# The last inverse stage of a long convolution with 64 output columns per weight: high and low constants side by side, low halves added in memory by accumulating GpSimd transfers

## The chip, the cores and the metric

The kernel runs on one core of a Trainium2 chip. The metric is the device time of one execution in microseconds (us), shown as the median of three runs. A profile is one more execution with the hardware profiler on. TensorE is PE in the rows (PEld is its weight load), VectorE is DVE, ScalarE is ACT, GpSimd is POOL, and SyncE, which only issues transfers here, is SP.

## What is computed

Four layers act on x (2048 rows, 576 columns), each with a residual and a row normalization ahead of it. Layers one and three are a Fourier mix; layers two and four multiply by the output of a branch that depends on the inputs k, v and the filters alone, so that it is computed once.

```
x = x + real(DFT_seq(DFT_hidden(layernorm(x))))       # dense DFT matrices
x = x + layernorm(x) * y                              # y: the branch
x = x + real(DFT_seq(DFT_hidden(layernorm(x))))
x = x + layernorm(x) * y

kv = conv4(k, shift_k) * v
y  = irfft(rfft(kv, 4096) * rfft(ssm_k, 4096))[:2048] + kv * ssm_D
```

## The kernel before

**Numbers.** All matrix products run on values rounded to a shorter mantissa (type fp32r). To keep the precision each operand is split into a high and a low part, and a product takes three matmuls: high by high, high by low, low by high. `split` (lines 97 to 99) makes the two parts: ACT copies the rounded high part, DVE subtracts.

**The main work.** `layer` (line 300) multiplies by the sequence DFT in 128 steps of 14 matmuls of 512 columns, with constants that are loaded and split as it goes (`load_c`, line 213; a ring of three buffers). Behind each block of 512 outputs come eight pieces of `hidden` (line 276), each 27 matmuls of 288 columns. The second Fourier layer is done by `strassen` and is not touched.

**The branch.** `branch` (line 349) is a generator. It is advanced between the parts of the first Fourier layer, by estimated costs (`work`, `total`, `spent`, lines 769 to 798): a row of the last stage counts `I2_COST` = 2.0 us. It has three stages. The first transforms (`f1_products`) and writes to memory (`t_d`). The middle takes 64 groups: `mid_half` transforms again, `mid_kernel` and `mid_signal` form the complex product in the columns of two tiles (`kk` and, before, a scratch tile `p2`), `mid_inverse` transforms back, evicts into a buffer of the ring `vo` and stores to `v_d`. The last stage, `i2_products` (line 551), makes 32 row tiles, 16 for each half of the 576 columns. One such **row** reads a tile of 128 partitions by 2 by 288 from `v_d`, splits it (`split_feed`, line 586), multiplies it with the constants `i2c` of this row, evicts 128 by 288 with one activation into a buffer of `vo` (three buffers, also used by the middle stage) and stores it to `yb_d` from the ACT queue.

**Where the rows stand.** The list `feeds` (lines 562 to 569) sets the order: 32 groups of the first half, groups of the second half with the first ten rows put between them (two groups to a row, from group 37 on), and then the last 22 rows without a group between them. The first stretch is called the mixed stretch below, the second the late stretch. After the last group `fc` and `land`, the rings of constants and of loaded tiles, go from two buffers to four (lines 634 to 643).

**What orders the engines.** The program is written as one list and a scheduler puts each engine's instructions into a fixed order; within an engine they run in that order. The function `act` (line 509) ties every ScalarE operation of the branch behind the previous one. Waits on buffers are semaphores. The constants of a row are loaded by `load_fr` (line 170) from GpSimd's queue, because that transfer also rounds. PSUM for the branch and for `hidden` are three banks in rotation (`bank`, line 83).

**Who reads the result.** `gated` (line 656) loads `yb_d[j]` from SP's queue for the second layer, and again for the fourth.

Of the kernel before, what the change touches and what calls it, by code (L numbers as in the profile page):

```python
# [10 lines left out]
F32 = mybir.dt.float32  # L11
# [4 lines left out]
P = 128  # L16
HP = P // 2
S = 2048
# [47 lines left out]
def fnet_h3_kernel(ctx: ExitStack, tc: tile.TileContext, x, c_mat, w_re, w_im, k_pad, v, shift_k,  # L66
# [7 lines left out]
    def mm(ps, lhsT, rhs, first, last, more=False):  # L74
        return nc.tensor.matmul(ps, lhsT, rhs, start=first, stop=last, skip_group_check=more).ins  # L75
# [7 lines left out]
    def bank():  # L83
        return psp.tile([P, NT], F32, tag="b", bufs=3, name="bk")
# [46 lines left out]
    def lay(t, at, *sizes):  # L131

        for name, words, n in sizes:
            ring.setdefault(name, Ring()).tiles.extend(t[:, at + i * words:at + (i + 1) * words] for i in range(n))
            at += n * words
        assert at <= t.shape[1], (at, t.shape, sizes)
        return at
# [28 lines left out]
    def load_after(dst, src):  # L166
        with tc.issue_after(anchor[-1]):
            return nc.sync.dma_start(dst, src).ins
# [30 lines left out]
        return t  # L199

    t_d = dr.tile([P, 2 * J, 2 * D], F32, name="td")
    v_d = [dr.tile([P, J, 2, HD], F32, name=f"vd{h}") for h in range(2)]
    yb_d = [dr.tile([P, D], F32, name=f"yb{j}") for j in range(J)]
    xa_d = [dr.tile([P, D], F32, name=f"xa{j}") for j in range(J)]
    xb_d = [dr.tile([P, D], F32, name=f"xb{j}") for j in range(J)]
# [140 lines left out]
    def quads(v):  # L346
        return v.rearrange("p (a q) -> p a q", a=4)

    def branch():
# [142 lines left out]
        at = lay(m1, at, ("yf", D, 2))  # L492
        fc_at = at
        at = lay(flts, SC_AT + CRAW * NT, ("res", D, 2))
        lay(flts, at, ("land", D, 2), ("kk", D, 2), ("vo", HD, 3), ("p2", HD, 1))
        mc = quads(ring["mc"]())
        load_fr(mc, midc)
        lo, hi = slice(0, 64), slice(64, 128)
# [10 lines left out]
        def act(*args, **kw):  # L509
            if last_act:  # L510
                with tc.issue_after(last_act[-1]):
                    last_act.append(nc.scalar.activation(*args, **kw).ins)  # L512
            else:
                last_act.append(nc.scalar.activation(*args, **kw).ins)
# [5 lines left out]
        def mid_kernel(df):  # L520
            pk, kk = mid_half(df, HD), two(ring["kk"]())
            act(kk[:, 0, :], pk[:, :HD], AF.Copy)
            act(kk[lo, 1, :], kk[hi, 0, :], AF.Copy)
            act(kk[hi, 1, :], kk[hi, 0, :], AF.Copy, scale=-1.0)
            act(kk[hi, 0, :], kk[lo, 0, :], AF.Copy)
            return kk

        def mid_signal(df, kk):
            px = mid_half(df, 0)
            p1, p2 = kk[:, 0, :], ring["p2"]()  # L530
            nc.vector.tensor_tensor(p1, px[:, :HD], p1, OP.mult)  # L531
            nc.vector.tensor_tensor(p2[lo], px[hi, :HD], kk[hi, 1, :], OP.mult)  # L532
            nc.vector.tensor_tensor(p2[hi], px[lo, :HD], kk[lo, 1, :], OP.mult)  # L533
            nc.vector.tensor_tensor(p1, p1, p2, OP.add)  # L534
            return p1

# [5 lines left out]
        def mid_inverse(hf, qg, yf):  # L542
            pv = bank()
            mm(pv[:, :HD], mc[:, 2, :], yf[:, 0, :], True, False)
            mm(pv[:, :HD], mc[:, 2, :], yf[:, 1, :], False, False)
            mm(pv[:, :HD], mc[:, 3, :], yf[:, 0, :], False, True)
            vo = ring["vo"]()
            act(vo, pv[:, :HD], AF.Copy)
            nc.scalar.dma_start(v_d[hf][4 * qg:4 * qg + 4].rearrange("q j c d -> (q j c) d"), vo)

        def i2_products(hf, j, fc, vf):
            yo = ring["vo"]()
            ps = bank()
            for c in range(2):
                cs = slice(c * HD, (c + 1) * HD)
                mm(ps[:, :HD], fc[:, c, :], vf[0][:, cs], c == 0, False)
                mm(ps[:, :HD], fc[:, c, :], vf[1][:, cs], False, False)
                mm(ps[:, :HD], fc[:, 2 + c, :], vf[0][:, cs], False, c == 1)
            act(yo, ps[:, :HD], AF.Copy)
            nc.scalar.dma_start(yb_d[j][:, hf * HD:(hf + 1) * HD], yo)  # L560

        mids = [(0, hf, qg) for hf in range(2) for qg in range(32)]
        late = [(1, 0, j) for j in range(J)]
# [10 lines left out]
        def load_feed(i):  # L574
            if i < len(feeds):
                kind, hf, q = feeds[i]
                landed[i] = ring["land"]()
                load_after(landed[i], v_d[hf][:, q].rearrange("p c d -> p (c d)") if kind else
                           t_d[4 * q:4 * q + 4, :, hf * D:(hf + 1) * D].rearrange("m j d -> (m j) d"))

        def load_fc(k):
            if k < len(rows):
                fcs[k] = quads(ring["fc"]())
                load_fr(fcs[k], i2c[rows[k]])

        def split_feed(i):
# [13 lines left out]
        for i, (kind, hf, q) in enumerate(feeds):  # L600
            df = halves.pop(i)
            if kind:
                i2_products(hf, q, fcs.pop(used), df)
                load_fc(used + ahead)
                used += 1
            else:
                if len(yfs) == MID_LAG:
                    mid_inverse(*yfs.pop(0))
                    yield 0.4
                kk = mid_kernel(df)  # L610
                if product is not None:
                    yfs.append((*product[:2], mid_round(product[2])))
                yield 1.6
                product = hf, q, mid_signal(df, kk)
            split_feed(i + 2)
            if i >= I2_FIRST - 8 and feed_ahead == 3:
                tiles = [ring["land"]() for _ in range(3)]
                if tiles[0] is third:
                    ring["land"], feed_ahead = Ring(tiles[1:]), 2
                    lay(m1, fc_at, ("fc", 4 * P, 2))  # L620
                    load_fc(0)
                    load_fc(1)
            if feed_ahead == 2:
                feed_ahead = 2.5
            else:
                load_feed(i + int(feed_ahead) + 2)
            if i == last_mid:
                yield 0.4
                mid_inverse(*yfs.pop(0))
                yfs.append((*product[:2], mid_round(product[2])))  # L630
                while yfs:
                    yield 0.4
                    mid_inverse(*yfs.pop(0))
                for name, t, at, words in (("fc", m1, spare, 4 * P), ("land", flts, kk_at, D)):
                    old = ring[name]
                    held = [old.tiles[(old.n + m) % 2] for m in range(2)]
                    fresh(name)
                    lay(t, at, (name, words, 2))
                    ring[name].tiles.extend(held)
                for m in range(2):  # L640
                    load_fc(used + ahead + m)
                    load_feed(i + ahead + 3 + m)
                ahead = feed_ahead = 4
            yield I2_COST if kind else 1.1
# [438 lines left out]
def _parts(a):  # L1083
    h = _r11(a)
    return h, _r11(a - h.astype(np.float64))


def _constants():
    p, q, j = np.arange(P), np.arange(P), np.arange(J)
    n = (32 * (p % HP) + J * (p // HP))[None, :, None] + j[:, None, None]  # L1090
    ang = 2 * np.pi * (n * (4 * q[None, None, :HP] + 1) % 8192) / 8192
    f1 = _parts(np.stack([np.cos(ang), -np.sin(ang)], axis=3).reshape(J, P, P))
    f1c = np.stack(f1, axis=2)
    n = (16 * p[None, :, None] + j[:, None, None]) * (4 * q[None, None, :] + 1) % 8192
    at = (2 * np.pi * n / 8192).transpose(0, 2, 1)
    at = at[:, np.concatenate([[2 * g, 2 * g + 1, HP + 2 * g, HP + 2 * g + 1] for g in range(HP // 2)])]
    i2 = [_parts(np.cos(at) / S), _parts(-np.sin(at) / S)]
    i2c = np.stack([i2[0][0], i2[1][0], i2[0][1], i2[1][1]], axis=2)
    w = np.arange(2 * J)
    th = 2 * np.pi * (w[:, None] * w[None, :] % (2 * J)) / (2 * J)  # L1100
    f2 = np.zeros((2, 2, 2 * J, 2, 2, 2 * J))
    i1 = np.zeros((2, 2, 2 * J, 2, 2, J, 2))
    c, s = np.cos(th), np.sin(th)
    for a in range(2):
        f2[a, 0, :, 0, a, :] = c
        f2[a, 1, :, 0, a, :] = s
        f2[a, 0, :, 1, a, :] = -s
        f2[a, 1, :, 1, a, :] = c
    th = 2 * np.pi * (j[:, None] * j[None, :] % J) / J
    c, s = np.cos(th), np.sin(th)  # L1110
    for a in range(2):
        for b in range(2):
            i1[0, a, b::2, b, a, :, 0] = c
            i1[1, a, b::2, b, a, :, 0] = -s
            i1[0, a, b::2, b, a, :, 1] = s
            i1[1, a, b::2, b, a, :, 1] = c
    m = [*_parts(f2.reshape(P, P)), *_parts(i1.reshape(P, P))]
    return f1c, i2c, np.stack(m, axis=1)

# [39 lines left out]
```

## Time and profile before

| | |
|---|---|
| median of 3 runs | 1193.91 us (1193.26 to 1196.67) |
| the profiled execution | 1195.03 us |
| its span (first to last instruction) | 1193.3 us |
| granted TensorE clock | 0.998 of full speed |
| instructions | 18055 |

The profiled execution lies 1.12 us above the median; 1.7 us of it are outside the span. In the rows, "L512" is a line of the kernel; since helpers issue most instructions, many kinds of work share a line: L75 is every matmul, L98 and L99 are `split`, L512 every ScalarE operation of the branch and L518 the subtraction in its splits. A row "out<-in" names the tiles: `flts` is a large tile that holds the rings of 32-bit buffers (`vo` among them), `mid` holds the rounded operands of the middle and last stage, `bk` are the three rotating banks, `s` and `rm` the accumulators of the main work, `mats` its operands.

### The profile page before, as it was taken

The page shows a single profiled execution, that of the slowest core. Times are in us where ns is not written, and L with a number is a line of the kernel's source. Part 1 is how long each engine was busy: PE and PEld are TensorE (multiplying, and loading weights), DVE is VectorE, ACT ScalarE, POOL GpSimd, SP SyncE. Part 2 cuts the span into 40 slices and gives each one's busy share as a digit, 9 for nine tenths or more (in the row PEclk, how much of TensorE's full clock was granted, in tenths as well). Part 3 has the DMA queues.
Part 4 walks back from the last instruction along what each step waited for, and adds up shares of the span by engine and source line. Part 5 has one row for each costly group of instructions (what it writes and reads, how often), then busy time and mean ns, then how long its engine had stood idle before and what let it go on. Part 6 is the DMA issues. An engine that isn't in the chain of part 4 may idle for free.

```text
span 1193.3 us, 18055 instructions
## 1 busy us (share of the span) xinstructions
PE 1172.4 (98%) x6248; PEld 996.3 (83%) x6248; DVE 840.3 (70%) x1498; ACT 661.1 (55%) x1311; POOL 75.6 (6%) x116
## 2 busy tenths in 40 slices
PE   7999999999999999999999999999999999999997
PEld 5776667888888888888988898888888888889997
DVE  7899983679777677685347756865776777774764
ACT  7865655679877668775435666634444445450210
POOL 2210000000000000001101121000000000001111
PEclk9999999999999999999999999999999999999999
DMA  9869898546666656648957676872672777895621
GB/s 327 306 199 311 263 295 269 167 133 188 217 194 211 206 174 203 207 133 272 295 193 236 230 246 226 267 260 71 220 277 76 220 278 258 248 334 158 217 86 41
DMA packets 142846, 259.85 MB, mean 218 GB/s; under 512 B 15649, under 2 KB 43553, under 8 KB 142754
## 3 DMA queue, kind: packets, MB, share of 16 engines
q1 hardware_dynamic: 102674, 205.45, 53.1%
q10 hardware_dynamic: 33168, 42.63, 10.3%
q0 software_dynamic: 6912, 10.62, 3.5%
q8 instruction: 49, 0.80, 0.3%
q14 instruction: 43, 0.35, 0.1%
HBM read 191.99 MB, written 66.65 MB: 217 GB/s over the span
## 4 chain that ended last, share of the span: by engine, by line
PE 76%; ACT 3%; DVE 1%; issue 1%; DMA 0%; POOLq 0%; ACTq 0%; DVEq 0%; SPq 0%
PE s L75 43%; PE bk L75 30%; PE rm L75 4%; ACT flts L512 1%; ACT mid L512 1%; ACT u L98 0%; DMA wd<-w 0%; ACT mats L98 0%; DVE mid L518 0%; DVE flts L534 0%; DVE flts L533 0%; DVE flts L531 0%; DVE flts L532 0%; DVE mats L99 0%; POOLq L1155 0%
## 5 line engine op out<-in xcount | busy, mean ns | idle before, releaser
L75 PE MATMUL s<-mats 128*128 128x512 f32 x2088 | 540.9, 395 | 2.4 <-DVE mats L99 0.8
L75 PEld LDWEIGHTS s<-mats 128*128 128x128 f32 x2088 | 380.9, 188 | 84.8 <-issue 10.4
L99 DVE TENSOR_TENSOR mats<-flts,mats 128x512 fp32r<-128x512 f32 x206 | 141.1, 689 | 63.8 <-ACT mats L98 62.5
L98 ACT ACTIVATE mats<-flts 128x512 fp32r<-128x512 f32 x206 | 128.5, 629 | 82.0 <-PE bk L75 35.0
L75 PE MATMUL bk<-mid 128*128 128x288 f32 x768 | 131.9, 298 | 2.4 <-ACT flts L512 1.6
L75 PEld LDWEIGHTS bk<-mid 128*128 128x128 f32 x768 | 116.9, 188 | 20.0 <-ACT flts L512 6.3
L75 PE MATMUL bk<-w,u 128*128 128x288 f32 x864 | 121.0, 296 | 0.4 <-DVE w L241 0.4
L75 PEld LDWEIGHTS bk<-w,u 128*128 128x128 f32 x864 | 117.5, 188 | 4.0 <-ACT flts L512 1.2
L518 DVE TENSOR_TENSOR mid<-flts,mid 128x576 fp32r<-128x576 f32 (+1 forms) x149 | 93.5, 628 | 34.9 <-ACT mid L512 30.9
L512 ACT ACTIVATE flts<-bk 128x288 f32<-128x288 f32 x160 | 62.1, 404 | 86.8 <-PE bk L75 77.7
L75 PE MATMUL rm<-mats 128*128 128x512 f32 x304 | 94.8, 391 | 0.0
L512 ACT ACTIVATE flts<-flts 64x288 f32<-64x288 f32 x192 | 85.0, 443 | 5.5
L512 ACT ACTIVATE mid<-flts 128x576 fp32r<-128x576 f32 (+1 forms) x148 | 80.4, 575 | 7.6 <-DMA flts<-td 3.2
L451 ACT ACTIVATE flts<-bf 128x384 f32<-128x384 f32 (+1 forms) x104 | 43.2, 463 | 45.6 <-PE bf L75 45.5
L287 DVE TENSOR_TENSOR flts<-flts,bk 128x288 f32<-128x288 f32 x48 | 21.8, 454 | 65.9 <-PE bk L75 65.8
L75 PE MATMUL bk<-mats 128*128 128x288 f32 (+1 forms) x376 | 67.8, 317 | 0.0
L75 PEld LDWEIGHTS rm<-mats 128*128 128x128 f32 x304 | 56.9, 188 | 12.3 <-DVE flts L273 0.2
L75 PE MATMUL s<-t,mats 128*128 128x512 f32 x264 | 64.9, 389 | 0.0
L184 POOL TENSOR_TENSOR flts<-flts 128x1 f32<-128x1 f32 x35 | 29.2, 834 | 522.0 <-DVE flts L183 520.0
L75 PE MATMUL bk<-mats,t 128*128 128x288 f32 (+1 forms) x368 | 59.3, 303 | 0.0
L75 PEld LDWEIGHTS bk<-mats 128*128 128x128 f32 x376 | 55.5, 188 | 3.4
L75 PEld LDWEIGHTS s<-t,mats 128*128 128x128 f32 x264 | 49.5, 188 | 10.3
(145 smaller groups left out, 1467.5 us busy)
## 6 DMA issues: line engine op xcount, KB each, us to landing
flts<-in_c_mat SPq DMA_DIRECT2D x148, 256.0 KB, 3.6
ph<-in_c_mat SPq DMA_DIRECT2D x54, 512.0 KB, 4.5
flts<-in_c_mat SPq DMA_DIRECT2D x30, 512.0 KB, 5.0
flts<-td SPq DMA_DIRECT2D x53, 288.0 KB, 3.0
td<-flts ACTq DMA_DIRECT2D x36, 384.0 KB, 4.5
vd<-flts ACTq DMA_DIRECT2D x64, 144.0 KB, 2.5
flts<-vd SPq DMA_DIRECT2D x32, 288.0 KB, 4.6
mid<-in_i2c POOLq DMA_DIRECT2D x32, 256.0 KB, 4.9
```

The costliest lines, as they stand in the source:

```text
L75: return nc.tensor.matmul(ps, lhsT, rhs, start=first, stop=last, skip_group_check=more).ins
L98: a = nc.scalar.activation(h, src, AF.Copy).ins
L99: return a, nc.vector.tensor_tensor(l, src, h.bitcast(F32), OP.subtract).ins
L184: pows.append(nc.gpsimd.tensor_tensor(rs, ve, mhalf, OP.pow).ins)
L287: added[:] = [nc.vector.tensor_tensor(r[:, cs], r[:, cs], ps[:, :HD], OP.add).ins]
L451: stored[:] = [nc.scalar.activation(so[:, i, :], ps[i], AF.Copy).ins]
L512: last_act.append(nc.scalar.activation(*args, **kw).ins)
L518: nc.vector.tensor_tensor(l, src, h.bitcast(F32), OP.subtract)
```

## The change

The last stage is factored in another way. Before, output position was 16p + j, both halves of a loaded tile went into the same 128 outputs, and each of two column groups took three matmuls (six in all, one bank, one eviction, one store). Now the position is 32p + q + 16i with 64 values of p: each half i of a loaded tile makes its own 64 outputs. The weight holds the high constants of these 64 in one half of its columns and the low constants in the other, so that one matmul makes high and low products at once, on different partitions. Per half there are two matmuls (with the high and with the low data), one bank and one eviction; per row four matmuls, two banks and two evictions. The high half of each evicted tile (64 partitions) is stored to every second row of `yb_d[j]` from the ACT queue; then the low half (the other 64 partitions) is added onto the same rows in memory by a transfer with an add, issued by GpSimd. Such a transfer has to wait until the plain store has landed, and a `vo` buffer is free again only when its accumulating transfer is done. `vo` has four buffers, the scratch `p2` is gone, and the signs in `mid_kernel` are swapped so that the product is formed in place. The constants of a row are half as large, `v_d` is laid out with 32 positions, and a row's load takes two pieces per partition.

```diff
-        lay(flts, at, ("land", D, 2), ("kk", D, 2), ("vo", HD, 3), ("p2", HD, 1))
+        lay(flts, at, ("land", D, 2), ("kk", D, 2), ("vo", HD, 4))
...
-            act(kk[lo, 1, :], kk[hi, 0, :], AF.Copy)
-            act(kk[hi, 1, :], kk[hi, 0, :], AF.Copy, scale=-1.0)
+            act(kk[lo, 1, :], kk[hi, 0, :], AF.Copy, scale=-1.0)
+            act(kk[hi, 1, :], kk[hi, 0, :], AF.Copy)
...
-            p1, p2 = kk[:, 0, :], ring["p2"]()
+            p1, p2 = kk[:, 0, :], kk[:, 1, :]
             nc.vector.tensor_tensor(p1, px[:, :HD], p1, OP.mult)
-            nc.vector.tensor_tensor(p2[lo], px[hi, :HD], kk[hi, 1, :], OP.mult)
-            nc.vector.tensor_tensor(p2[hi], px[lo, :HD], kk[lo, 1, :], OP.mult)
+            nc.vector.tensor_tensor(p2[lo], px[hi, :HD], p2[lo], OP.mult)
+            nc.vector.tensor_tensor(p2[hi], px[lo, :HD], p2[hi], OP.mult)
...
         def i2_products(hf, j, fc, vf):
-            yo = ring["vo"]()
-            ps = bank()
-            for c in range(2):
-                cs = slice(c * HD, (c + 1) * HD)
-                mm(ps[:, :HD], fc[:, c, :], vf[0][:, cs], c == 0, False)
-                mm(ps[:, :HD], fc[:, c, :], vf[1][:, cs], False, False)
-                mm(ps[:, :HD], fc[:, 2 + c, :], vf[0][:, cs], False, c == 1)
-            act(yo, ps[:, :HD], AF.Copy)
-            nc.scalar.dma_start(yb_d[j][:, hf * HD:(hf + 1) * HD], yo)
+            cols = slice(hf * HD, (hf + 1) * HD)
+            late = []
+            for i in range(2):
+                ps, yo = bank(), ring["vo"]()
+                cs = slice(i * HD, (i + 1) * HD)
+                mm(ps[:, :HD], fc[:, i, :], vf[0][:, cs], True, False)
+                mm(ps[:, :HD], fc[:, i, :], vf[1][:, cs], False, True)
+                act(yo, ps[:, :HD], AF.Copy)
+                to = yb_d[j][i::2, cols]
+                nc.scalar.dma_start(to, yo[i * HP:(i + 1) * HP])
+                late.append((to, yo[(1 - i) * HP:(2 - i) * HP]))
+            for to, corr in late:
+                nc.gpsimd.dma_start(to, corr, accum_op=OP.add)
...
-                load_after(landed[i], v_d[hf][:, q].rearrange("p c d -> p (c d)") if kind else
+                load_after(two(landed[i]) if kind else landed[i], v_d[hf][:, q::J, :] if kind else
...
-                fcs[k] = quads(ring["fc"]())
+                fcs[k] = two(ring["fc"]())
```

The constants `i2c` (now 128 by 2 by 128 for a row) and the inverse matrices of the middle stage are built on the host to match.

More of the change, by code (lines that the diff above doesn't have):

```diff
@@ L201, in fnet_h3_kernel @@
     t_d = dr.tile([P, 2 * J, 2 * D], F32, name="td")
-    v_d = [dr.tile([P, J, 2, HD], F32, name=f"vd{h}") for h in range(2)]
+    v_d = [dr.tile([P, 2 * J, HD], F32, name=f"vd{h}") for h in range(2)]
     yb_d = [dr.tile([P, D], F32, name=f"yb{j}") for j in range(J)]
@@ L548, in mid_inverse @@
             act(vo, pv[:, :HD], AF.Copy)
-            nc.scalar.dma_start(v_d[hf][4 * qg:4 * qg + 4].rearrange("q j c d -> (q j c) d"), vo)
+            nc.scalar.dma_start(v_d[hf][4 * qg:4 * qg + 4].rearrange("m j d -> (m j) d"), vo)
         def i2_products(hf, j, fc, vf):
-            yo = ring["vo"]()
-            ps = bank()
-            for c in range(2):
-                cs = slice(c * HD, (c + 1) * HD)
-                mm(ps[:, :HD], fc[:, c, :], vf[0][:, cs], c == 0, False)
-                mm(ps[:, :HD], fc[:, c, :], vf[1][:, cs], False, False)
-                mm(ps[:, :HD], fc[:, 2 + c, :], vf[0][:, cs], False, c == 1)
-            act(yo, ps[:, :HD], AF.Copy)
-            nc.scalar.dma_start(yb_d[j][:, hf * HD:(hf + 1) * HD], yo)
+            cols = slice(hf * HD, (hf + 1) * HD)
[11 more added lines that the diff above has]
+                nc.gpsimd.dma_start(to, corr, accum_op=OP.add)
         mids = [(0, hf, qg) for hf in range(2) for qg in range(32)]
@@ L619, in branch @@
                     ring["land"], feed_ahead = Ring(tiles[1:]), 2
-                    lay(m1, fc_at, ("fc", 4 * P, 2))
+                    lay(m1, fc_at, ("fc", 2 * P, 2))
                     load_fc(0)
@@ L633, in branch @@
                     mid_inverse(*yfs.pop(0))
-                for name, t, at, words in (("fc", m1, spare, 4 * P), ("land", flts, kk_at, D)):
+                for name, t, at, words in (("fc", m1, spare, 2 * P), ("land", flts, kk_at, D)):
                     old = ring[name]
@@ L1093, in _constants @@
     f1c = np.stack(f1, axis=2)
[L1094 to L1098, printed above, removed]
+    n = np.arange(HP)[None, :] * 32 + np.arange(2 * J)[:, None]
+    at = 2 * np.pi * (n[:, None, :] * (4 * q[None, :HP, None] + 1) % 8192) / 8192
+    i2 = _parts(np.stack([np.cos(at) / S, -np.sin(at) / S], axis=2).reshape(2 * J, P, HP))
+    i2c = np.stack([np.concatenate([i2[0][:J], i2[1][:J]], axis=2),
+                    np.concatenate([i2[1][J:], i2[0][J:]], axis=2)], axis=2)
     w = np.arange(2 * J)
@@ L1101, in _constants @@
     f2 = np.zeros((2, 2, 2 * J, 2, 2, 2 * J))
-    i1 = np.zeros((2, 2, 2 * J, 2, 2, J, 2))
+    i1 = np.zeros((2, 2, 2 * J, 2, 2, 2 * J))
     c, s = np.cos(th), np.sin(th)
@@ L1108, in _constants @@
         f2[a, 1, :, 1, a, :] = c
[L1109 to L1116, printed above, removed]
+        i1[0, a, :, a, 0, :] = c
+        i1[1, a, :, a, 0, :] = -s
+        i1[0, a, :, a, 1, :] = s
+        i1[1, a, :, a, 1, :] = c
     m = [*_parts(f2.reshape(P, P)), *_parts(i1.reshape(P, P))]
```

## The prediction

> **What bounds the kernel now.** I read the page's busy times first, then its chain, then the stretches in which the branch's last stage runs.
>
> ```profile
> PE 1172.4 (98%) x6248; PEld 996.3 (83%) x6248; DVE 840.3 (70%) x1498; ACT 661.1 (55%) x1311; POOL 75.6 (6%) x116
> ...
> PE 76%; ACT 3%; DVE 1%; issue 1%; DMA 0%; POOLq 0%; ACTq 0%; DVEq 0%; SPq 0%
> PE s L75 43%; PE bk L75 30%; PE rm L75 4%; ACT flts L512 1%; ACT mid L512 1%; ACT u L98 0%; DMA wd<-w 0%; ACT mats L98 0%; DVE mid L518 0%; DVE flts L534 0%; DVE flts L533 0%; DVE flts L531 0%; DVE flts L532 0%; DVE mats L99 0%; POOLq L1155 0%
> ```
>
> PE is busy 98% of the span and holds 76% of the chain; nothing else holds more than 3%. Busy overlaps in pipelined matmuls, so the price of one matmul is read from the chain in order of time, where a piece is counted once (start, us, what):
>
> ```profile
> 569.55 0.79 PE bk L75 x6
> 570.35 2.08 PE s L75 x9
> 572.43 0.79 PE bk L75 x6
> ```
>
> Six matmuls of 288 columns take 0.79 us, 0.132 each; nine of 512 take 2.08, 0.231 each. The pieces follow each other without a gap: a matmul removed here is time removed, as long as nothing else comes late.
>
> The rows' evictions are `flts<-bk` of L512. The first and last row's store show the mixed stretch; the first, third, fifth and last of the 22 evictions show the late one:
>
> ```profile
> L560 ACTq DMA_DIRECT2D yb<-flts x10: 326/326/354, 390.7 to 501.6; - x10
> ...
> 551.58 0.41 ACT L512 ACTIVATE flts<-bk 128x288 f32<-128x288 f32 x1 [3.41 <-PE bk L75]
> 554.41 0.41 ACT L512 ACTIVATE flts<-bk 128x288 f32<-128x288 f32 x1 [0.97 <-PE bk L75]
> 554.72 0.68 ACT L512 ACTIVATE mid<-flts 128x576 fp32r<-128x576 f32 x1
> 554.86 0.33 ACTq L560 DMA_DIRECT2D yb<-flts  x1
> 558.95 0.41 ACT L512 ACTIVATE flts<-bk 128x288 f32<-128x288 f32 x1 [1.60 <-DMA yb<-flts]
> 608.99 0.41 ACT L512 ACTIVATE flts<-bk 128x288 f32<-128x288 f32 x1 [1.69 <-PE bk L75]
> ```
>
> The first ten rows come one in (501.6 - 390.7)/9 = 12.3 us. The last 22 come one in (608.99 - 551.58)/21 = 2.73 us. A store is issued 0.45 us after its eviction starts (554.41 to 554.86). And once, at 558.95, the eviction already waits 1.60 us until a store has left its `vo` buffer: the ring of three is close to binding now. The two stretches as a whole (us, busy of PE, PEld, DVE, ACT, POOL; clock, DMA share, GB/s):
>
> ```profile
> 551.50:609.50 58.00, 58.00 (x353) 52.66 (x352) 22.17 (x32) 24.78 (x50) 9.51 (x18) 1.00 0.87 277
> 384.00:551.50 167.50, 166.38 (x927) 145.11 (x928) 120.20 (x232) 120.60 (x262) 6.33 (x12) 1.00 0.63 190
> ```
>
> **The change part by part.**
>
> *Matmuls.* Each row loses two of six: 32 x 2 x 0.132 = -8.4 us on a PE that never waits in these stretches, 2.64 in the mixed and 5.81 in the late one.
>
> *Evictions.* 32 more at 0.41 us are 13 us of ACT, which is idle 33 of 58 us in the late stretch and 47 of 167 in the mixed one. Cost nothing; where ACT could not hide them, it would be at most 22 x 0.41 = 9 us late and 4 mixed. A row also takes two of the three rotating banks; the next row's second bank needs the previous row's first eviction, which is a wait on the ring below rather than one of its own.
>
> *GpSimd's queue.* It gets 64 transfers. Those it issues now cost it 9.5 us for 18, 0.53 each; three to a row are 1.6 us, below 2.73. Cost nothing as work; it is the waits that matter.
>
> *Constants, loads, scratch.* Constants fall by 128 KB a row (4 MB in all) and the accumulates add 4.7 MB written, and the same read again; the row loads come in twice as many pieces. The loads are asked four rows ahead in the late stretch, so a longer landing stays hidden: nothing, bounded by one row's 2.73 us. In-place products in the middle stage keep the same instructions: nothing.
>
> *The wait that comes in.* In the order in which the changed kernel is built, every eviction of a row waits, besides PE, for the accumulating transfer of the eviction four before it. So a `vo` buffer goes round a loop: eviction, issue of the plain store, its landing, issue of the accumulate, its landing, next eviction. A row uses two buffers of four, so two rows share one loop of length L. In the mixed stretch two middle groups use the other two buffers, so a row's buffer comes back after a whole row, 12.3 us. In the late stretch two rows take 5.5 us now. What is queued behind the waiting eviction on ACT is all that PE lives on: the split of the next row, tied behind it, and the splits of the main work's constants, which have only three buffers. PE's order is fixed too: it stops at the next row's bank. So the late stretch goes at the pace of the loop.
>
> The trace has no accumulating transfer. Its nearest rows are the plain stores of rows and the transfers that GpSimd issues (min/median/max us to landing; 144, 256 and 128 KB, ten in the mixed stretch, 22 and 18 in the late one):
>
> ```profile
> L560 ACTq DMA_DIRECT2D yb<-flts x10: 326/326/354, 390.7 to 501.6; - x10
> DMA to landing us min/median/max: 1.9/3.4/6.3
> ...
> L172 POOL DMA_DIRECT2D mid<-in_i2c x10: 527/527/530, 390.5 to 501.4; - x10
> DMA to landing us min/median/max: 3.1/3.7/6.1
> ...
> L560 ACTq DMA_DIRECT2D yb<-flts x22: 326/327/830, 552.4 to 609.4; - x22
> DMA to landing us min/median/max: 1.8/4.9/7.8
> ...
> L172 POOL DMA_DIRECT2D mid<-in_i2c x18: 527/528/532, 551.8 to 597.9; - x18
> DMA to landing us min/median/max: 3.2/5.6/8.2
> ...
> L172 POOL DMA_DIRECT2D f1r<-in_f1c x15: 527/528/692, 5.6 to 155.5; - x15
> DMA to landing us min/median/max: 2.7/3.8/6.7
> ```
>
> Landings grow with the DMA share (0.63 and 0.87). If the late stretch takes 92 us instead of 58, its 277 GB/s become 175, and with 22 x 144 KB written and read less 22 x 128 KB of constants 175 to 215, near the mixed stretch's 190. So I take the mixed medians: 3.4 us for a store, 3.7 for the accumulate, whose half-sized rows against a read of the destination more I set off against each other; 128 instead of 256 KB made no difference (3.8). In the built order a row's second store stands behind the next row's split (0.68 us on ACT), so for the second buffer L = 0.45 + 0.68 + 3.4 + 3.7 = **8.2 us**. Ends: 0.45 + 1.9 + 3.1 = 5.45 (mixed minima, no split in between) and 0.45 + 0.68 + 4.9 + 5.6 = 11.6 (late medians).
>
> *The sum.* The 22 evictions start 0.88, 1.95, 1.95, 2.59, 5.83, 0.88, 2.11, 2.61, 2.88, 5.51, 0.88, 2.77, 2.64, 6.94, 0.88, 1.91, 2.85, 2.87, 5.51, 0.88 and 2.09 us apart; the long gaps are the 27-matmul pieces. Take 0.26 from each gap, and let a row start no earlier than L after the row two before it. With L = 8.2 the starts run 0, 0.6, 8.2, 9.9, 16.5, 22.0, ... 83.3, 86.3, 91.6 instead of 57.4: +34.2. Less 2.64 in the mixed stretch and the last row's 0.26: **+31 us**. On the profiled 1195.03 that is 1226.3; that execution is 1.12 above the median, so 1225 as a median. Without the wait the same list gives 51.9, and -8.4 in all; at L = 5.45 it gives 68.7 (+8.4), at 11.6 it gives 121.9 (+61.6). It breaks even near L = 4.2.
>
> *A page against it.* The Trainium skill, "DMA: Bandwidth & Descriptors", section "Rules for kernel authors", advises against splitting a transfer into two disjoint partition halves, since both use the same engines and serialize. By that the two stores of a row would land later than one did, and the sum would move toward the longer loop; no run here shows it.
>
> The next layer's first read of `yb` comes after the late stretch and takes rows that were stored first, so the last accumulates delay nothing:
>
> ```profile
> L168 SPq DMA_DIRECT2D flts<-yb x10: 319/352/430, 613.3 to 1109.7; - x10
> ```
>
> **The rivals.**
>
> 1. *The loop is short.* Halved stores land like the quickest of now: L = 5.45, 68.7 us, 1202 as a median. For it: minima of 1.8 and 2.7 exist. Against it: medians are nearly twice that, and the loop needs two landings in a row, of both buffers, eleven times. By the fit in "DMA: Bandwidth & Descriptors" of the Trainium skill, section "Anatomy of one DMA — SWDGE (gpsimd) path", 2.0 us plus bytes at 436 GB/s, 72 KB would land in 2.2 us; the estimate by it is a loop of 5.5 us and the same 1202. The trace does not bear it out: 144 KB took 3.4 and 4.9.
> 2. *The wait is covered* (the other side: faster). If two rows' loop stays under 4.2 us, the saved matmuls win; fully covered, the time is 1193.9 - 8.4 = 1185.5. Place: the late evictions. Against it: eviction and two minima alone make 0.45 + 1.8 + 2.7 = 4.95.
> 3. *The loop is long.* Accumulates read and write memory, and GpSimd's queue is in order: before many second accumulates stands a load of constants that waits for the products of a later row, so that an accumulate waits for PE, which waits for evictions. With L = 11.6 or more: 1255 and above. Against it: a longer stretch thins the traffic.
>
> That the change does not do what it says I rule out: in the built order each row has two banks with two matmuls each.
>
> **How the numbers follow.** Forecast (L about 6.5 to 10): 0.62. Short loop: 0.16. Covered: 0.05. Long: 0.17. About 0.3% (3.6 us) can be told from no change here. Of the short case 0.02 lies within that; so faster 0.05, same 0.02, slower 0.93. The range reaches from just under the short case, 1200, to the long case's 1255 and leaves out the covered case and most of what is beyond.
>
> **What would show it.** 6184 matmuls of PE; 64 accumulates on POOL. ACT's evictions of L512 waiting for transfers of `yb` by tens of us in the late stretch; PE idle there, 30 us and more, where it has none now; the stretch about 92 us long, the mixed one about 2.6 shorter, the rest unchanged. Two stores and two accumulates per row, whose landings sum to some 7 us. The prediction is wrong if the late evictions still wait for PE, if landings sum to under 4 us, or if new idle time stands outside the late stretch.

## The result, and the profile after

The changed kernel takes 1222.4 us (median of six runs, 1220.16 to 1227.15) against 1195.5 us of the kernel before beside it (1193.26 to 1197.66): a ratio of 1.0232, 95% interval 1.0208 to 1.0255, or 27 us slower. The profiled execution is the slowest of the six, 1227.15 us with a span of 1225.4; against the 1195.03 and 1193.3 of before that is 32.1 us, and the comparison of the two traces has to find these 32.1.

From the page of the changed kernel: busy times, the chain that ended last, and two groups of instructions (busy us, mean ns, then the idle time just before them and what ended it).

```profile
span 1225.4 us, 18167 instructions
...
PE 1179.6 (96%) x6184; PEld 992.8 (81%) x6184; DVE 839.0 (68%) x1498; ACT 671.8 (55%) x1343; POOL 130.6 (11%) x180
...
PE 47%; DMA 8%; DVE 3%; ACT 2%; issue 2%; POOL 0%; ACTq 0%; POOLq 0%; DVEq 0%; SPq 0%
...
L512 ACT ACTIVATE flts<-bk 128x288 f32<-128x288 f32 x192 | 74.4, 405 | 104.5 <-DMA yb<-flts 47.3
...
L564 POOL DMA_DIRECT2D yb<-flts x64 | 54.0, 899 | 88.2 <-DMA yb<-flts 37.8
```

PE has 64 matmuls fewer, 6184, and yet lost its place as the only bound: DMA, which showed 0% of the chain before, holds 8%. The evictions of L512 waited 47.3 us for transfers of `yb`, the wait that the change brought in.

Where in the span it lies, by stretches (busy of PE, PEld, DVE, ACT, POOL; granted clock, DMA share, GB/s):

```profile
384.00:549.00 165.00, 163.26 (x900) 141.08 (x900) 119.17 (x230) 122.41 (x271) 23.55 (x32) 1.00 0.67 191
549.00:643.00 94.00, 75.47 (x363) 60.32 (x362) 26.56 (x39) 36.98 (x78) 45.65 (x61) 0.91 0.85 191
643.00:1225.00 582.00, 568.95 (x2953) 493.96 (x2951) 387.55 (x688) 242.80 (x431) 36.91 (x50) 0.99 0.63 206
```

The second row is the late stretch. In it PE is idle for 18.5 of 94 us; the same stretch before, in the prediction, shows no idle time (58.00 busy of 58.00). The third row holds idle time too: 13.1 us, where its counterpart before (611 to 1193 us) has 7.4. The first late eviction, the first eviction of row 21 (ten loops of four evictions on) and that of row 22:

```profile
549.58 0.71 ACT L512 ACTIVATE flts<-bk 128x288 f32<-128x288 f32 x2 [2.88 <-DMA flts<-vd]
...
634.87 0.41 ACT L512 ACTIVATE flts<-bk 128x288 f32<-128x288 f32 x1 [2.27 <-DMA yb<-flts]
...
638.22 0.41 ACT L512 ACTIVATE flts<-bk 128x288 f32<-128x288 f32 x1
```

So the late stretch starts 2.0 us earlier than before (549.58 for 551.58) and takes 88.6 us from the first row to the last instead of 57.4, that is 31.2 more. What follows the last row's first eviction is 2.9 longer (1225.4 - 638.22 = 587.2 for 584.3), and this is the difference of two terms, which the last store of `out` from ACT's queue divides. Before and after:

```profile
1188.72 0.38 ACTq L739 DMA_DIRECT2D out<-ph  x1
```

```profile
1215.65 0.39 ACTq L743 DMA_DIRECT2D out<-ph  x1
```

Up to that store it is 2.3 us shorter (577.4 for 579.7), in part because one step of 14 main matmuls has moved into the late stretch (136 matmuls of `s` and `rm` from the stretch's start to its last 27-matmul piece, for 122). From that store to the end of the span it is 5.2 longer (9.8 for 4.6). The sum, -2.0 + 31.2 - 2.3 + 5.2, is 32.1. The 5.2 us at the end are no part of the loop; the last section comes back to them.

One loop of a buffer, from the chain in order of time (start, us, what; a DMA piece is a transfer in flight, from its issue to its landing):

```profile
556.87 0.42 ACT flts L512
557.29 0.02 issue
557.31 4.42 DMA yb<-flts
561.73 0.02 issue
561.75 0.04 POOLq L564
561.79 0.47 issue
...
562.28 3.42 DMA yb<-flts
...
565.77 0.42 ACT flts L512
```

Eviction, store in flight for 4.42 us, GpSimd's sequencer about half a microsecond, accumulate in flight for 3.42, next eviction: 8.9 us, of which the chain gives 0.42 to ACT and nothing to PE. The mean over ten loops is (634.87 - 549.58)/10 = 8.5. Landings in the late stretch, stores first, then accumulates:

```profile
L561 ACTq DMA_DIRECT2D yb<-flts x44: 452/453/577, 550.0 to 640.8; - x44
DMA to landing us min/median/max: 1.9/3.3/5.1
...
L564 POOL DMA_DIRECT2D yb<-flts x43: 802/827/1391, 553.2 to 642.8; - x43
DMA to landing us min/median/max: 2.5/3.8/5.6
```

### The profile page after: what moved, and what is told of

It is laid out like the page before. It is cut to its first block, busy times and chain, and to the rows that moved or that the text cites. A ratio compares the mean times of both kernels' runs of the same rounds, so it can differ in the third digit from the quotient of the medians.

```text
span 1225.4 us, 18167 instructions
## 1 busy us (share of the span) xinstructions
PE 1179.6 (96%) x6184; PEld 992.8 (81%) x6184; DVE 839.0 (68%) x1498; ACT 671.8 (55%) x1343; POOL 130.6 (11%) x180
## 4 chain that ended last, share of the span: by engine, by line
PE 47%; DMA 8%; DVE 3%; ACT 2%; issue 2%; POOL 0%; ACTq 0%; POOLq 0%; DVEq 0%; SPq 0%
PE s L75 28%; PE bk L75 18%; DMA yb<-flts 6%; PE rm L75 2%; ACT flts L512 1%; DVE mats L99 1%; DMA t<-ud 1%; ACT mats L98 0%; DMA flts<-td 0%; DMA flts<-vd 0%; DVE flts L181 0%; ACT u L98 0%; DMA y<-flts 0%; ACT mid L512 0%; DVE gate L669 0%
## 5 line engine op out<-in xcount | busy, mean ns | idle before, releaser
L75 PE MATMUL s<-mats 128*128 128x512 f32 x2088 | 546.8, 396 | 2.2 <-ACT mats L195 0.8
L75 PEld LDWEIGHTS bk<-mid 128*128 128x128 f32 x704 | 109.7, 189 | 47.3 <-ACT flts L512 23.5
L512 ACT ACTIVATE flts<-bk 128x288 f32<-128x288 f32 x192 | 74.4, 405 | 104.5 <-DMA yb<-flts 47.3
L75 PE MATMUL bk<-w,u 128*128 128x288 f32 x864 | 124.2, 300 | 2.0 <-ACT w L240 1.0
L75 PEld LDWEIGHTS bk<-w,u 128*128 128x128 f32 x864 | 120.6, 192 | 6.6 <-ACT flts L512 2.9
L512 ACT ACTIVATE flts<-flts 64x288 f32<-64x288 f32 x192 | 85.0, 443 | 5.7 <-ACT flts L512 0.3
L512 ACT ACTIVATE mid<-flts 128x576 fp32r<-128x576 f32 (+1 forms) x148 | 80.1, 574 | 5.6 <-DMA flts<-td 2.1
L75 PEld LDWEIGHTS rm<-mats 128*128 128x128 f32 x304 | 57.4, 189 | 11.9 <-issue 0.2
L564 POOL DMA_DIRECT2D yb<-flts x64 | 54.0, 899 | 88.2 <-DMA yb<-flts 37.8
```

The lines of the kernel that those rows point to most:

```text
L564: nc.gpsimd.dma_start(to, corr, accum_op=OP.add)
```

## The experiments

The theory is that of the prediction: the late stretch goes at the pace of the loop of a `vo` buffer, two landings in a row. Two rivals give the same 27 us in other ways: the memory or the DMA engines are full with adds, or GpSimd's queue, in order and with each add waiting for its store, is the pace. Ratios are to the kernel before, run beside each on the same chip.

### More buffers: eight in the late stretch

Four more `vo` buffers are put where the later `land` buffers stood; `land` and `fc` get other room.

```diff
-                for name, t, at, words in (("fc", m1, spare, 2 * P), ("land", flts, kk_at, D)):
+                for name, t, at, words in (("fc", m1, spare - 4 * P, 2 * P), ("land", m1.bitcast(F32), spare, D)):
...
+                held = [ring["vo"]() for _ in range(4)]
+                fresh("vo")
+                lay(flts, kk_at, ("vo", HD, 4))
+                ring["vo"].tiles.extend(held)
```

> The changed kernel with eight vo buffers instead of four in the late stretch (the buffers kk leaves are used for vo, and the later loads go to space that the middle stage leaves). Loop theory: four rows share one loop of about 8.9 us, 2.2 us a row, less than PE needs (2.47), so the late stretch falls from 89 us to 53 to 60 and the time to 1185 to 1196 us. Rival 'memory': the accumulates' traffic sets the pace (DMA share 0.85 there): no gain, 1215 us and more. Rival 'GpSimd queue': two accumulates of 0.83 us and a load of 0.6 in order, with waits for stores and for PE between them, set the pace: 1200 to 1215 us.

1206.34 us, ratio 1.0095 (1.0077 to 1.0114). Sixteen of the 27 us go with the number of buffers. Ten over the kernel before stay, which the loop alone does not give: by it, 1196 was the most, and the result lies in the range given for GpSimd's queue (1200 to 1215). About five of the ten are the end of the program: up to the last store of `out` the profiled execution is 4.8 us behind the kernel before (1193.49 for 1188.72). For the rest, eight buffers still wait for transfers of `yb`, and the DMA engines are full (the DMA share, last but one in the row, is 1.02). Waits and the window from 549 to 615 us:

```profile
ACT flts L512 <- DMA yb<-flts: 17.1, 11, 3.1
...
POOL yb L564 <- DMA yb<-flts: 6.5, 4, 2.9
```

```profile
549.00:615.00 66.00, 55.88 (x313) 47.67 (x312) 21.62 (x32) 31.15 (x70) 41.77 (x57) 1.00 1.02 245
```

### Fewer buffers: three

```diff
-        lay(flts, at, ("land", D, 2), ("kk", D, 2), ("vo", HD, 4))
+        lay(flts, at, ("land", D, 2), ("kk", D, 2), ("vo", HD, 3))
```

> The changed kernel with three vo buffers instead of four. Loop theory: one and a half rows share a loop of 8.9 us, 5.9 us a row, 21 rows take 125 us instead of 89: about 1258 us (1245 to 1270). Rivals 'memory' and 'GpSimd queue': the number of buffers does not matter much, 1222 to 1232 us.

1245.26 us, ratio 1.0419 (1.0404 to 1.0435): at the lower end of what the loop gave, 13 us short of its middle, and well outside both rivals. Three, four and eight buffers make 1245, 1222 and 1206. The loop with three was shorter than assumed: the traffic was thinner (171 GB/s from 549 to 665 us, where four buffers had 191 in their late stretch), and the landings were shorter (stores, then accumulates, over the whole late stretch):

```profile
L561 ACTq DMA_DIRECT2D yb<-flts x44: 452/453/523, 554.2 to 661.6; - x44
DMA to landing us min/median/max: 1.9/2.5/4.4
L564 POOL DMA_DIRECT2D yb<-flts x43: 802/815/1455, 557.4 to 661.2; - x43
DMA to landing us min/median/max: 2.5/3.3/5.4
```

2.5 + 3.3 where four buffers had 3.3 + 3.8. I read this as a feedback, slower evictions thinning the traffic that they wait for; at any rate the loop's length is not a constant that can be carried from one buffer count to another.

### One landing instead of two: adds onto a tensor that nothing reads

With four buffers, the accumulates go to `yc_d`, so that none waits for a store; the result then lacks the low parts.

```diff
+    yc_d = [dr.tile([P, D], F32, name=f"yc{j}") for j in range(J)]
...
-                late.append((to, yo[(1 - i) * HP:(2 - i) * HP]))
+                late.append((yc_d[j][i::2, cols], yo[(1 - i) * HP:(2 - i) * HP]))
```

> The changed kernel, but the accumulating transfers add onto a scratch tensor in memory that nobody reads, so the low parts are missing from the result and an accumulate no longer waits until the plain store has landed. All transfers and their bytes stay. Loop theory: the two landings lie side by side, the loop is 0.45 + 0.5 + 0.7 + 3.8 = 5.5 us, the list of the late stretch gives 69 us, about 1203 us. Rival 'memory' (adding in memory is dear as such): within 5 us of the changed kernel's 1222. Rival 'GpSimd queue': 1210 to 1222, since its order and its work are the same.

1210.87 us, ratio 1.0128 (1.0113 to 1.0143): 11.5 us come back. That is above the loop's 1203 and just inside the range for GpSimd's queue (1210 to 1222). No theory had the longer end of the program; with its 5.2 us the loop would have given 1208. A part of the loss is left over that has nothing to do with the order behind the store.

### The low half added on chip

Four matmuls per row as in the change, but ScalarE copies the low half from the bank across partitions into `vo` and VectorE adds the high half; one plain store per half, no accumulate.

```diff
+            yo = ring["vo"]()
...
-                act(yo, ps[:, :HD], AF.Copy)
...
-                late.append((to, yo[(1 - i) * HP:(2 - i) * HP]))
-            for to, corr in late:
-                nc.gpsimd.dma_start(to, corr, accum_op=OP.add)
+                act(yo[high], ps[low, :HD], AF.Copy)
+                nc.vector.tensor_tensor(yo[high], yo[high], ps[high, :HD], OP.add)
+                nc.scalar.dma_start(yb_d[j][i::2, cols], yo[high])
```

> The changed kernel's four matmuls per row, but no transfer adds: ScalarE copies the low half from the bank to the high half's partitions in a vo buffer (64 partitions), VectorE adds the high half from the bank, and the sum is stored once from the ACT queue; one vo buffer per row. Loop theory: with one landing in the loop and four rows in it nothing binds, and 64 matmuls of 0.132 us are saved: 8.4 us below the kernel before, about 1186 us (1184 to 1190). If the second bank and eviction of a row cost something that the waits hid: 1190 to 1196. If VectorE's 64 extra adds come late: above the kernel before.

1194.24 us, ratio 0.9987 (0.9975 to 0.9999). The whole loss goes with the accumulating transfers, while matmuls, banks, two evictions a row (now of 64 partitions) and two-piece loads stay: these cost nothing that would explain a slower kernel. Five microseconds of what goes are the end of the program, which is as short again as before (1191.5 - 1186.89 = 4.6 us). But most of the expected gain of 8.4 us failed to come, and the result lies in the range given for the case that the second bank and eviction cost something (1190 to 1196); that is left open. The late stretch still waited for stores, three times, up to 5.1 us:

```profile
ACT flts L512 <- DMA yb<-flts: 12.0, 3, 5.1
```

### What eight buffers still cost: wait or add

Four kernels with eight buffers, one of which is the run above, differ only in whether the low half's transfer waits for the store (same rows) or not (the unread tensor), and whether it adds or plainly writes. On the unread tensor the low parts are missing from the result; a plain write over the same rows leaves the low parts alone. The edit for the one without either; the other two each take one of the two lines:

```diff
-                late.append((to, yo[(1 - i) * HP:(2 - i) * HP]))
+                late.append((yc_d[j][i::2, cols], yo[(1 - i) * HP:(2 - i) * HP]))
...
-                nc.gpsimd.dma_start(to, corr, accum_op=OP.add)
+                nc.gpsimd.dma_start(to, corr)
```

Neither wait nor add:

> The kernel with eight vo buffers (1206 us, DMA share 1.02 in its late stretch), but the low halves go from GpSimd's queue as plain transfers to a scratch tensor that nobody reads: no add in memory, the low parts are missing from the result. GpSimd issues as many transfers. Theory: with the loop gone the DMA engines are the next floor, and an adding transfer costs them some 0.59 us of all sixteen where a plain one costs 0.26 (q0 less the constants, against q10): 42 x 0.33 = 14 us of DMA time go, 70 becomes 56, and the time falls by 8 to 12 us, to 1194 to 1198. Rival 'GpSimd queue' (issue work and order): within 3 us of 1206.

Add without wait:

> The changed kernel with eight vo buffers, whose low halves are added by GpSimd onto a tensor that nothing reads, so that no add waits for a store; the low parts are missing from the result. It has the adding transfer without the wait, where the run of eight buffers (1206.3) has both and the one with plain transfers onto that tensor (1194.9) neither. If the wait for the store is what eight buffers still cost, it comes near 1195 (1192 to 1198). If the adding transfers cost it by themselves (longer on the engines, longer to issue), it comes near 1206 (1203 to 1209). Halfway means that both do.

Wait without add:

> The changed kernel with eight vo buffers, whose low halves are written by GpSimd onto the same rows by a plain transfer instead of added, so that the order behind the store stays and the add goes; the result holds the low parts alone. It has the wait without the adding transfer. If the wait for the store is what eight buffers still cost, it comes near 1206 (1203 to 1209). If the adding transfers cost it by themselves, near 1195 (1192 to 1198). Together with the run onto the unread tensor it makes the four cases of wait and add: the two differences from 1194.9 should sum to about 11.5 if the causes are independent.

| eight buffers | no wait for the store | wait |
|---|---|---|
| plain transfer | 1194.88, ratio 0.9998 (0.9989 to 1.0008) | 1202.42, 1.0048 (1.003 to 1.0066) |
| adding transfer | 1201.88, 1.0041 (1.0028 to 1.0053) | 1206.34, 1.0095 (1.0077 to 1.0114) |

Both middle cases lie between the corners, clear of either, as had been set for two causes; so each costs by itself: by the ratios 0.43 points for the add and 0.50 for the wait, together 0.93 of the 0.97 that separate the corners, within the intervals. As medians they are 7.0 and 7.5 us against 11.5 for both, so that whether the two simply add up is not settled. All four kernels have as many transfers from GpSimd, so their number alone is not what makes the difference between them. With plain transfers and no wait the kernel is level with the one before, but not all along: up to the last store of `out` its profiled execution is 5.4 us ahead (1183.35 for 1188.72), and the longer end of the program takes that back.

What the add itself costs shows between the two kernels without the wait. GpSimd's issues and landings to 613 us, and its queue of the DMA engines in the window from 549 to 615 (packets, MB, share of the 16 engines); plain first, then adding:

```profile
L565 POOL DMA_DIRECT2D yc<-flts x44: 521/527/547, 551.0 to 605.8; - x44
DMA to landing us min/median/max: 2.0/4.4/6.6
...
q0 software_dynamic: 4144, 5.74, 31.2%
```

```profile
L565 POOL DMA_DIRECT2D yc<-flts x42: 802/1340/2337, 553.2 to 610.9; - x42
DMA to landing us min/median/max: 3.6/6.0/8.0
...
q0 software_dynamic: 6112, 5.61, 49.5%
```

For about the same bytes the queue took 49.5% of 66 us of all engines, 32.7 us, where plain transfers took 20.6; each of the 44 adds costs 0.27 us of all 16 engines more (0.33 had been estimated). GpSimd needed 1.34 us for an issue instead of 0.53, and a landing took 6.0 instead of 4.4 us. PE's granted clock differs too, 1.00 with plain transfers and 0.97 with adds in that window. Which of these costs the 7 us the runs do not tell apart: they come together.

### Does lighter DMA traffic help: rows loaded in one piece

The positions of `v_d` are permuted on the host's constants so that a row's load has one piece of 2304 bytes per partition again, in three kernels: with the add on chip, the same with eight buffers, and the changed kernel's accumulates with eight buffers.

```diff
-                load_after(two(landed[i]) if kind else landed[i], v_d[hf][:, q::J, :] if kind else
+                load_after(landed[i], v_d[hf][:, 2 * q:2 * q + 2, :].rearrange("p c d -> p (c d)") if kind else
```

> The add on the chip (1194 us), with the 32 positions of v_d in another order (columns of the inverse constants permuted on the host), so that a row's load is one piece of 2304 bytes per partition again instead of two of 1152. Theory: the saved matmuls of the late stretch were eaten by loads that came late, since two pieces cost 4.8 us more DMA time in that stretch: 1188 to 1192 us. Rival: the second bank and eviction of a row eat them: 1193 to 1195.

> As before it (add on the chip, loads in one piece), and eight vo buffers in the late stretch, against the 12 us that ScalarE's evictions still waited there for the stores of yb. Theory: nothing but PE binds then; all 64 matmuls show, 1186 to 1190 us. Rival 'second bank': no better than with four buffers.

> The accumulating transfers with eight vo buffers (1206 us) and the row loads in one piece. Theory (DMA engines are the floor there, 70 us of work in 69): 4.8 us of DMA time less, so 1200 to 1203 us. Rivals 'GpSimd queue' and loop: no change, 1205 to 1208.

1192.53 (0.9966, 0.9954 to 0.9979), 1190.99 (0.9962, 0.9949 to 0.9974) and 1208.03 (1.0104, 1.009 to 1.0118). The first two beat the kernel before by 0.3 to 0.4%, and both came out just above their ranges (1188 to 1192 and 1186 to 1190). Between them the intervals overlap, so that what the eight buffers add is not shown and the rival of the second bank is not ruled out. The third came out at the rivals' no change, not at the 1200 to 1203 of a floor by DMA time: the share of SyncE's queue, which carries the loads, fell (41.4% to 38.0% from 549 to 615 us), and the time did not. It is not a clean case, since PE's granted clock was 0.95 in that window where two-piece loads had 1.00, and some of the gain may have gone there. Its waits from 549 to 615 us are the same two as with two-piece loads, and no shorter:

```profile
ACT flts L512 <- DMA yb<-flts: 18.9, 13, 3.5
POOL yb L564 <- DMA yb<-flts: 9.6, 8, 3.2
```

That agrees with the four cases, in which the wait for a store costs time without the add.

## Why the prediction was right

The forecast was 1225 us with a loop of 8.2 us as the mechanism; measured are 1222.4 and a mean loop of 8.5. The mechanism is borne out; that the number came so near is partly luck. The forecast had no term for the end of the program, where 5.2 us of the profiled 32.1 lie. If the other executions end alike, some 22 of the 27 us between the medians are left for the stretches that the +31 was worked out for. One of the prediction's own signs of being wrong, new idle time outside the late stretch, came with it. Point by point:

- **The loop sets the pace.** Shown for most of the loss, by the chain, by three buffer counts in order and by taking away the order behind the store. The list of gaps with L = 8.2 gave 91.6 us for the late stretch; it took 88.6. The three microseconds are the last step: row 21 came at 85.3 for a forecast 86.3, row 22 at 3.35 us behind it where the list put 5.3.
- **Its terms.** Landings were taken as 3.4 and 3.7 from plain transfers of 144 and 256 KB; the halves, 72 KB each, took 3.3 and 3.8. The 0.68 of a split between eviction and store is absent from the loop shown from the chain. In its place stand some 0.5 us of GpSimd between the store's landing and the accumulate, which the prediction had left out. Two errors of opposite sign.
- **Matmuls removed.** 6184, as predicted; the earlier start of the late stretch is 2.0 us of a predicted 2.64. The other 5.81 cannot show under the loop. Where the loop is gone they show only in part: the best kernel gains 5.0 us of 8.4 (1190.99 against 1195.97 of the kernel before beside it). In its late stretch, 549 to 608 us, PE shows 1.0 us of idle time, and ACT still waited for two stores:

```profile
549.00:608.00 59.00, 58.01 (x337) 50.96 (x336) 42.74 (x78) 36.70 (x73) 9.50 (x18) 1.00 0.82 234
```

```profile
ACT flts L512 <- DMA yb<-flts: 6.7, 2, 3.8
```

  Where the rest of the 8.4 went stays open; it was not tried further.
- **Evictions, banks, loads, in-place products: nothing.** Not refuted and not shown: with adds on chip all of them are there and the kernel is not slower, but some of the gain that failed to come may be theirs. The two-piece loads were worth 0.2% there (0.9987 to 0.9966, with intervals that overlap a little).
- **GpSimd's issue work at 0.53 each: nothing.** The size was off: an accumulate's issue takes 0.83 us (median 827 ns), and GpSimd was busy 45.65 of 94 us instead of the 9.51 before. In the loop shown that is about half a microsecond. Under eight buffers and without the wait the adds cost 7 us of their own.
- **PE idle by 30 us and more.** 18.5 us. PE was also granted only 0.91 of its clock there, by estimate 8.5 of the 94 us, and one step of main matmuls more ran in the stretch.
- **The rest unchanged.** The end of the program is 5.2 us longer, below. No term stood for it.
- **The rivals.** The short loop and the covered wait were wrong because landings had the medians of their neighbours, not the minima. The long loop's mechanism, GpSimd's queue in order, is there (loads of constants in it waited 12.6 us for PE in all); the mean loop stayed at 8.5 all the same, and what the queue added to it was not separated. The rule on disjoint partition halves in the Trainium skill, "DMA: Bandwidth & Descriptors", section "Rules for kernel authors", would have made the second store late; the halves landed in 3.3 us where whole rows had taken 4.9 at a higher rate, and no run here separates halves from traffic. The fit of that page, 2.2 us for 72 KB, is not borne out under this load: plain transfers of 72 KB from GpSimd, the path that it is given for, took 2.0 us at best and 4.4 in the median with eight buffers.

## What to carry to other kernels

Before a buffer's release is moved to a later transfer, walk its loop once: eviction, every landing in series and the issue between them, divided by the number of buffers, against the time that the consumer now takes per buffer. Count an add in memory as a transfer of more than its bytes, on the engines, on the issuing queue and in flight; an add on VectorE, which had time to spare, did the same without any of that. A saved matmul is worth its duration only where nothing else in that stretch comes within that duration of being late. And compare the two traces up to the last store as well as to their ends: here the end alone held 5 us, and it made a kernel that was ahead look level.

## What was not expected of the hardware

**The program ends later.** From ACT's last store of `out` to the end of the span pass 9.4 to 9.8 us in all eight kernels in which GpSimd transfers the low halves, and 4.5 to 4.7 in the four others: the kernel before, and the three with the add on chip. Plain transfers do it as well as adding ones (1192.8 - 1183.35 = 9.45), so it is not the add. The last landings of `out` come some 2 us after their issue; behind them the profile shows nothing, so what takes the time stays open. The kernel before has 48 transfers from GpSimd too, all of them loads; whether the number of transfers counts or their direction was not tried.

**PE's clock fell in the late stretch.** The granted clock there was 0.91, and in windows of 20 us (the fields are as above) it fell further towards the end:

```profile
610.00:630.00 20.00, 16.42 (x78) 12.77 (x77) 5.70 (x8) 7.78 (x17) 9.38 (x13) 0.91 0.92 222
630.00:650.00 20.00, 17.36 (x75) 14.67 (x76) 5.27 (x10) 6.03 (x13) 6.56 (x8) 0.83 0.69 145
```

Closer up it is 0.50 for six microseconds:

```profile
636.00:642.00 6.00, 5.76 (x23) 5.23 (x23) 3.42 (x5) 3.68 (x8) 1.93 (x3) 0.50 0.52 79
```

The 27-matmul piece that lies there, behind the last row's matmuls, after and before:

```profile
636.84 6.20 PE L75 MATMUL bk<-w,u 128*128 128x288 f32 x27 [0.24 <-ACT flts L512]
```

```profile
610.64 3.77 PE L75 MATMUL bk<-w,u 128*128 128x288 f32 x27
```

It takes 2.4 us more, at a place where the loop no longer covers it. In the kernel before, whose PE does not wait in this stretch, the clock stayed at 1.00; so it looks as if waits of PE were paid twice, once as idle time and once as slower matmuls, but no run tests that by itself. The Trainium skill, "TensorE: Matmul & The Clock Gate", section "HAM oscillation — how this bites in real kernels", describes that PE drops to half its clock when its waits on DMA, 3 to 5 us each in the case there, cross a window of 3.4 us. The trace agrees in the half clock; but the longest wait of PE in this stretch was 1.9 us (total, times, longest):

```profile
PE bk L75 <- ACT flts L512: 12.1, 13, 1.9
PE bk L75 <- ACT mid L512: 6.3, 7, 1.9
```

How much PE is idle does not decide it alone: from 549 to 615 us the run with eight buffers was idle for 10.1 us at a clock of 1.00, and the one with loads in one piece and accumulates for 7.1 us at 0.95.

**A neighbour of the fourth buffer.** The four `vo` buffers reach into the room of another tile, and an activation right behind the stretch waited for the last accumulate:

```profile
649.18 0.60 ACT L272 ACTIVATE flts<-rm 64x512 f32<-64x512 f32 x1 [8.39 <-DMA yb<-flts]
```

PE did not wait for it, since it had other work through all of it (7.00 of 7.00 us busy):

```profile
643.00:650.00 7.00, 7.00 (x33) 5.77 (x32) 0.65 (x2) 0.60 (x1) 1.46 (x2) 1.00 0.85 229
```
